# Masks from VectorE, two banks with different head placement, and another order of the first steps in a retention and feed-forward kernel

## The chip, the cores and the metric

The kernel runs on one core of one Trainium2 chip. The metric is device time in microseconds (us) of one execution. Before the change it is 185.12 us, the median of three runs (185.02 to 185.44).

## The reference

Four sequences of 768 tokens, 8 heads of 64. Each head keeps a 64 x 64 state that decays by a factor per step:

```python
gamma = 1.0 - 2.0 ** (-5.0 - np.arange(H))
for t in range(S):
    state = gamma * state + outer(k[:, :, t], v[:, :, t])
    y[:, :, t] = scale * q[:, :, t] @ state
x = y as (3072 tokens, 512)
a = x @ w1;  b = x @ w2            # 512 -> 1024
out = ((a * b) @ w3) @ w_out       # 1024 -> 1024 -> 512
```

Everything goes in and comes out as float32.

## The kernel before

**Tiling.** The 768 tokens of a sequence are cut into three chunks of 256 (`T`, `PER`), so there are 12 chunks, n = 0 to 11. `w3` and `w_out` are multiplied once into a 1024 x 512 matrix `W3O`, so that a chunk needs three products: with W1, with W2 and with W3O. All products run in float16 with float32 sums. The first two chunks (`EO` = 2) hold tokens in pairs per partition and are split in two halves; the later ones are split in four subchunks (s, g), two banks g of two halves s.

**One chunk of attention.** `scores` (L335) makes k times q per subchunk; `mask` (L346, L352) multiplies it on VectorE with a triangle of ones, `keep` or `keep64`, into `am`. `kv` (L374) makes k times v; `state` adds it up on VectorE, and its last step multiplies the end state by the decay of 256 steps, `GS`, on GpSimd (L62). `inter` (L425) writes state times q into two PSUM banks X[n, 0] and X[n, 1], and `av` (L450) adds `am` times v into the same banks. Both are made of small products of 64 rows and 64 columns, so that the 128 x 128 array holds four of them: a row half (the partitions that the operands lie in) and a column half (the partitions that the output goes to). In `inter` head parity r gives both: row half r, column half r. In `av` the row half is g, the column half r. Between the two stands `fence` (L438), a copy on ScalarE of a few columns of each bank, so that `av` starts in a bank only when `inter` is done there. `x_out` (L467; L462 for chunks 0 and 1) multiplies each bank by a table of decays, `YN` or `YS`, into `XT`, one VectorE instruction a bank.

**Numbers and tables.** `numbers` and `late_numbers` write indices with iota on GpSimd, and after them, on GpSimd too: logarithms of the decays by 16 memsets of one column (`LGH`, `LGP`, L148 and L149), the masks by memset and affine selects (`keep`, L152 to L156, and `keep64`, L169 to L172), and `GS` by 8 memsets (L210). VectorE multiplies and converts (`arguments`, `late_arguments`), ScalarE takes exponentials (`tables`, `late_tables`; YN by 4 instructions).

**One chunk of the feed-forward part.** `two_blocks` (L484) makes a quarter of a or b for 256 tokens, 8 products of 256 columns. `a_evac` copies a out of PSUM on ScalarE (L59); `b_evac` multiplies it by b on VectorE into `HT` (L62). `o_unit` (L532) multiplies HT by W3O, 8 products of 512 columns per 128 tokens, and `o_copy` (L546) takes it out on ScalarE. `rows` (L514) is the same work as `two_blocks` for chunks 0 and 1, cut by rows of w1 and w2, so that it can start when the first rows are there.

**W3O.** Per row block f of w3: `cast_w3` to float16, `turn_w3` (8 transposes, L236), `turned_w3` out of PSUM, `w3_mm(f, i)` (2 products of 512 columns with quarter i of w_out, L248; `cast_wo` casts that quarter), `w3_out`. `warm` (L565) multiplies zeros, only to keep TensorE busy.

**What sets the order.** The schedule is manual: each engine executes its instructions in the order in which the program issues them, and waits by semaphores. Up to chunk 4's attention, the order is a list written out by hand (L572 to L841); then a loop over n = 3 to 11 (L879) issues, for each n: `inter(n)`, `fence(n)`, scores and kv of n + 1, `av(n)`, `x_out`, states and masks of n + 1, transposes of chunk n + 2 and loads of chunk n + 3, output products of n - 1, and four units of `two_blocks` and evacuations. Loads come from SP's queue in the order of a list, `fetch` (L120), into 15 buffers of 512 KB: r is a row block of w3, wo a quarter of w_out, w1 and w2 followed by a digit their quarters of rows, q, k and v followed by a digit a chunk. Later chunks' k and q are transposed by DMA, from SP too (`dma_turn`, L295), after a cast on GpSimd.

Of the kernel before, what the change touches and what calls it, by code (L numbers as in the profile page):

```python
# [20 lines left out]
def kernel(  # L21
# [44 lines left out]


# [40 lines left out]
    def fetch(names):  # L108
# [12 lines left out]
        "r3 r6 wo0 r5 q0 r4 wo2 k0 wo1 wo3 r2 v0 r1 r7 k1 q1 v1 w12 w11 r0 w10 w13 w23 w20 w21 w22 "  # L121
        "v2 q2 k2 q5 k3 k4 q3 q4 v3"
# [10 lines left out]
    LGP = const.tile([128, NP], FP, name="LGP")  # L133
    keep = const.tile([128, 2, 128], FP, name="keep")
# [4 lines left out]
    def numbers():  # L139

        nc.gpsimd.iota(key_i[:, :, :], pattern=[[1, 2], [0, H]], base=1 - 128, channel_multiplier=2)
        nc.gpsimd.iota(
            col_i[:, :, :].rearrange("p g (t j) -> p g t j", t=2), pattern=[[128, 2], [1, 2], [2, 64]],
            base=1 - 128, channel_multiplier=0,
        )
        for h in range(H):
            r = (h % 2) * 64
            nc.gpsimd.memset(LGH[:, h : h + 1], -math.log(gam[h]))  # L148
            nc.gpsimd.memset(LGP[r : r + 64, h // 2 : h // 2 + 1], math.log(gam[h]))  # L149

    def keeps():
        nc.gpsimd.memset(keep[:, :, :], 1.0)  # L152
        for g in range(2):
            rows = slice(g * 64, g * 64 + 64)
            for t in range(2):
                nc.gpsimd.affine_select(  # L156
                    out=keep[rows, t, :], in_=keep[rows, t, :], compare_op=GE, fill=0.0,
                    base=-t, pattern=[[1, 2], [2, 64]], channel_multiplier=-2,
                )

    def late_numbers():
# [7 lines left out]
        nc.gpsimd.memset(keep64[:, :], 1.0)  # L169
        for g in range(2):  # L170
            rows = slice(g * 64, g * 64 + 64)
            nc.gpsimd.affine_select(  # L172
                out=keep64[rows, :], in_=keep64[rows, :], compare_op=GE, fill=0.0,
                base=0, pattern=[[1, 2], [2, 32]], channel_multiplier=-1,
            )
# [5 lines left out]
    GS = const.tile([128, NP, 64], FP, name="GS")  # L181
# [13 lines left out]
    def identity():  # L195
        make_identity(nc, ident16[:, :])
# [10 lines left out]
    def step_decays():  # L207
        for h in range(H):
            r, p = (h % 2) * 64, h // 2
            nc.gpsimd.memset(GS[r : r + 64, p, :], gam[h] ** T)  # L210

    def late_arguments():
        tt("v", vn_x[:, :, :], tok_i[:, :, :], lgh(), MULT)
        copy("v", pos_f[:, :, :, :], pos_i[:, :, :, :])

    def late_tables():
        nc.scalar.activation(VN[:, :, :], vn_x[:, :, :], AF.Exp)
        for p in range(NP):
            nc.scalar.activation(YN[:, :, p, :, :], pos_f[:, :, :, :], AF.Exp, scale=LGP[:, p : p + 1])

# [91 lines left out]
    def half(x):  # L312
        return slice(x * 64, x * 64 + 64)

# [63 lines left out]


# [4 lines left out]
    def state(n, i, eng="g"):  # L384
# [3 lines left out]
        if i == len(cs) + 1:  # L388
            if n % PER < PER - 1:
                TS[n + 1, cs[0] if n + 1 < EO else (0, 0)] = t = att.tile([128, NP, 64], HP, tag="t0", name="t0")  # L390
                tt(eng, t[:, :, :], TS.pop((n, "end"))[:, :, :], GS[:, :, :], MULT)
# [18 lines left out]
    def inter(n, tags):  # L410
# [4 lines left out]
        for a in range(NP):  # L415
            for c in cs:
                if (n, c) not in TS:
                    continue
# [13 lines left out]
    def fence(n):  # L432

        for g in range(2):
            if (g, 0) in X[n]:
                s0 = 0 if n < EO or (n, (0, g)) in TS else 1
                t = att.tile([128, NP, 2 - s0], FP, tag=f"fence{g}", name="fence")
                nc.scalar.copy(t[:, :, :], X[n, g][:, :, :].rearrange("p a (s i) -> p a s i", s=2)[:, :, s0:, 0])  # L438

    def av(n):  # L440
        begun = X.pop(n)
        for a in range(NP):
            for t in range(2):
                for g, r in QUARTERS:
# [3 lines left out]
                    else:  # L448
                        o, rhs = X[n, g][half(r), a, t * 64 : (t + 1) * 64], am[n, None, r][half(g), a, t, :]
# [6 lines left out]
    def x_out(n, g):  # L456
# [9 lines left out]
        else:  # L466
            nc.vector.tensor_tensor(  # L467
                XT[n][:, :, :].rearrange("p a (s x) -> p (a s) x", s=2)[:, :, g * 64 : (g + 1) * 64].rearrange(
                    "p k (i t) -> p k t i", t=2
                ),  # L470
                x[:, :, :].rearrange("p a (s t i) -> p (a s) t i", s=2, t=2),
                YN[:, g, :, :, :].rearrange("p a s (t i) -> p (a s) t i", t=2), MULT,
            )
# [100 lines left out]
    identity()  # L574
    step_decays()
    late_numbers()
    numbers()
    warm(3, "F2")
    cast_w3(3, "v")
    turn_w3(3, "S0")  # L580
    keeps()
    late_arguments()
    warm(9, "F2")
    arguments()
    late_tables()
    turned_w3(3, "v")
    cast_w3(6, "g")
    cast_wo(0, "v")
    tables()
    turn_w3(6, "S0")  # L590
    cast_w3(5, "g")
    w3_mm(3, 0, "S1", first=True)
    turned_w3(6, "v")
    w3_mm(6, 0, "S0", first=True)
    turn_w3(5, "X0")
    cast("q", 0, "v")
    warm(2, "F2")
    turned_w3(5, "s")
    turn("q", 0, "X1")
    cast_w3(4, "v")  # L600
    w3_mm(5, 0, "X0", first=True)
    turned("q", 0, "v")
    turn_w3(4, "K")
    warm(3, "F2")
    cast_wo(2, "s")
    turned_w3(4, "v")
    w3_mm(4, 0, "X1", first=True)
    w3_mm(6, 2)
    w3_mm(3, 2)
    cast("k", 0, "v")  # L610
    w3_mm(5, 2)
    turn("k", 0, "K")
    w3_mm(4, 2)
    cast_wo(1, "s")
    turned("k", 0, "v")
    scores(0, ("K", "F0"), 0)
    cast_wo(3, "s")
    w3_mm(4, 1)
    mask(0, 0, 0)
    w3_mm(3, 1)  # L620
    mask(0, 1, 0)
    w3_mm(6, 1)
    cast_w3(2, "s")
    w3_mm(4, 3, last=True)
    w3_mm(3, 3, last=True)
    w3_out(4, "v")
    w3_mm(5, 3)
    w3_out(3, "s")
    turn_w3(2, "K")
    cast_v(0, "v")  # L630
    w3_mm(6, 3, last=True)
    turned_w3(2, "s")
    w3_mm(5, 1, last=True)
    scores(0, ("S1", "X1"), 1)
    w3_out(5, "v")
    kv(0, ("F0", "F1"))
    w3_out(6, "s")
    w3_mm(2, 1, "K", first=True)
    mask(0, 1, 1)
    w3_mm(2, 2)  # L640
    w3_mm(2, 3)
    cast_w3(1, "v")
    cast_w3(7, "s")
    w3_mm(2, 0, last=True)
    state(0, 1)
    turn_w3(1, "S0")
    w3_out(2, "s")
    mask(0, 0, 1)
    inter(0, ("X0", "X1"))
    turn_w3(7, "F0")  # L650
    turned_w3(1, "v")
    fence(0)
    cast("k", 1, "s")
    av(0)
    state(0, 2)
    w3_mm(1, 0, "S0", first=True)
    state(0, 3)
    x_out(0, 0)
    turned_w3(7, "s")
    turn("k", 1, "S1")  # L660
    x_out(0, 1)
    w3_mm(1, 2)
    w3_mm(1, 1)
    cast("q", 1, "s")
    turned("k", 1, "v")
    w3_mm(7, 1, "X0", first=True)
    w3_mm(7, 3)
    turn("q", 1, "S1")
    cast_v(1, "v")
    w3_mm(7, 2)  # L670
    turned("q", 1, "s")
    w3_mm(7, 0, last=True)
    cast_w(W1, "w1", 2, "g")
    kv(1, ("X1", "K"))
    w3_out(7, "s")
    w3_mm(1, 3, last=True)
    state(1, 1)
    scores(1, ("S1", "F0"), 1)
    state(1, 2)
    w3_out(1, "s")  # L680
    scores(1, ("X0", "X1"), 0)
    cast_w(W1, "w1", 1, "g")
    mask(1, 0, 1)
    inter(1, ("F1", "F2"))
    rows(W1, 0, 1, 2, ("S0", "K"), first=True)
    fence(1)
    mask(1, 0, 0)
    state(1, 3)
    rows(W1, 0, 1, 1)
    cast_w3(0, "s")  # L690
    mask(1, 1, 0)
    rows(W1, 0, 0, 1, ("S1", "X0"), first=True)
    rows(W1, 0, 0, 2)
    mask(1, 1, 1)
    turn_w3(0, "X1")
    cast_w(W1, "w1", 0, "v")
    av(1)
    turned_w3(0, "s")
    rows(W1, 0, 1, 0)
    x_out(1, 0)  # L700
    rows(W1, 0, 0, 0)
    x_out(1, 1)
    w3_mm(0, 1, "X1", first=True)
    w3_mm(0, 3)
    cast_w(W1, "w1", 3, "v")
    cast_w(W2, "w2", 3, "g")
    rows(W1, 1, 0, 2, ("F0", "F1"), first=True)
    rows(W1, 1, 0, 1)
    rows(W1, 1, 0, 3)
    cast_w(W2, "w2", 0, "v")  # L710
    w3_mm(0, 0)
    w3_mm(0, 2, last=True)
    rows(W1, 0, 1, 3, last=True)
    w3_out(0, "s")
    rows(W1, 0, 0, 3, last=True)
    rows_out("a", 0, 1, 1, "v")
    cast_w(W2, "w2", 1, "s")
    rows(W2, 1, 0, 0, ("X1", "F2"), first=True)
    rows(W2, 1, 0, 3)
    rows_out("a", 0, 0, 1, "v")  # L720
    rows(W1, 1, 0, 0, last=True)
    rows_out("a", 0, 0, 0, "s")
    cast_w(W2, "w2", 2, "v")
    rows(W2, 1, 1, 1, ("X0", "K"), first=True)
    rows_out("a", 1, 0, 1, "s")
    rows(W2, 1, 0, 1)
    rows_out("a", 1, 0, 0, "v")
    rows_out("a", 0, 1, 0, "s")
    rows(W2, 0, 1, 2, ("S1", "F1"), first=True)
    rows(W2, 1, 1, 2)  # L730
    cast_v(2, "v")
    rows(W2, 0, 0, 1, ("S0", "F0"), first=True)
    rows(W2, 0, 0, 3)
    rows(W2, 0, 0, 2)
    rows(W2, 0, 1, 3)
    cast("q", 2, "g")
    rows(W2, 0, 0, 0, last=True)
    rows(W2, 1, 1, 3)
    rows_out("b", 0, 0, 1)
    rows(W2, 0, 1, 0)  # L740
    rows(W2, 0, 1, 1, last=True)
    rows_out("b", 0, 0, 0)
    turn("q", 2, "F0")
    cast("k", 2, "g")
    rows_out("b", 0, 1, 0)
    rows(W2, 1, 1, 0, last=True)
    rows(W2, 1, 0, 2, last=True)
    turned("q", 2, "v")
    rows(W1, 1, 1, 3, ("S0", "S1"), first=True)
    rows_out("b", 1, 0, 1)  # L750
    rows(W1, 1, 1, 0)
    cast("q", 5, "g")
    rows(W1, 1, 1, 1)
# [201 lines left out]
```

## Time and profile before

| | |
|---|---|
| three runs, median | 185.12 us |
| profiled execution | 185.08 us |
| its span on the core | 183.3 us |
| TensorE busy / weight loads | 175.6 / 126.2 us |
| VectorE, ScalarE, GpSimd busy | 102.3, 67.2, 52.5 us |
| `inter`, chunks 4 to 11, one | 0.56 us, 0.43 in chunks 6 and 9 |
| `x_out`, chunks 2 to 11, one bank | 0.72 us |
| first load landed, first w3 product | 4.7 us, 10.45 us |
| start of the loop's first unit | 74.1 us |

The profile has a page (busy time, share in slices, the chain of work that ended last) and a trace that can be asked for windows, engines and waits. In a row of the timeline stand the start and the duration in us, the engine, the line of the kernel, the operation, what it wrote and read with its shape, a count, and in brackets how long the engine stood idle before it and what ended that. PE is TensorE, PEld its weight loads, DVE VectorE, ACT ScalarE, POOL GpSimd, SPq the queue of SyncE. In the chain a row is a start, a duration, an engine and what it wrote, with the line. A load of 512 KB is 128 rows of 4 KB for weights, but runs of 512 bytes for q and the first chunks, and of 256 bytes for k and v from chunk 2 on.

### The profile page before, as it was taken

What the parts mean: (1) busy time and instruction counts of PE and PEld (TensorE: products, weight loads), DVE (VectorE), ACT (ScalarE), POOL (GpSimd) and SP (SyncE); (2) the same over time, 40 slices, a digit from 0 to 9 for tenths busy, and PEclk for the clock granted to TensorE, in tenths of its full rate; (3) what the DMA queues carried; (4) which work ended last, traced back from release to release, by engine and by line L of the source; (5) the groups of instructions that cost most, each with busy time, mean ns of one, the idle gap of its engine ahead of it and who ended that gap; (6) DMA issues with size and microseconds to landing.
All of it is one profiled execution on the core that took longest, in us unless ns stands there. A gap on an engine that the chain in (4) does not pass through costs nothing.

```text
span 183.3 us, 5995 instructions
## 1 busy us (share of the span) xinstructions
PE 175.6 (96%) x2609; PEld 126.2 (69%) x2609; DVE 102.3 (56%) x173; ACT 67.2 (37%) x126; POOL 52.5 (29%) x82
## 2 busy tenths in 40 slices
PE   7779999999999999999999999999999999999993
PEld 2345455778965875885877858868688587784872
DVE  0544697867595495748357384464654836634320
ACT  2537477626062422332314314233233231331322
POOL 7830004420334005254435334434433400000000
PEclk9969999999999999999999999999999999999999
DMA  5999999996989999689899999999999991200203
GB/s 189 378 361 385 357 287 393 408 320 177 248 193 277 167 181 204 143 186 242 164 251 160 242 180 249 261 206 239 268 229 217 333 382 64 90 28 5 114 0 114
DMA packets 83578, 40.76 MB, mean 222 GB/s; under 512 B 61408, under 2 KB 78048, under 8 KB 83552
## 3 DMA queue, kind: packets, MB, share of 16 engines
q1 hardware_dynamic: 83552, 40.38, 88.0%
q8 instruction: 20, 0.33, 0.8%
q14 instruction: 6, 0.05, 0.1%
HBM read 29.36 MB, written 6.29 MB: 194 GB/s over the span
## 4 chain that ended last, share of the span: by engine, by line
PE 91%; POOL 4%; DVE 1%; issue 1%; ACT 0%; POOLq 0%
PE psF L484 34%; PE psF L532 19%; PE psX L248 4%; PE psS L248 3%; PE psS L514 3%; PE psX L425 3%; PE psF L514 2%; PE psX L532 2%; PE psS L532 2%; PE psX L484 2%; PE psX L450 2%; PE psX L514 1%; PE psS L484 1%; PE psS L335 1%; PE psK L248 1%
## 5 line engine op out<-in xcount | busy, mean ns | idle before, releaser
L484 PEld LDWEIGHTS <-w 128*128 128x128 f16 x640 | 62.5, 98 | 9.4 <-DVE xt L467 0.2
L484 PE MATMUL psF<-xt,w 128*128 128x256 f16 x576 | 64.4, 273 | 0.0
L62 DVE TENSOR_TENSOR ht<-pa,psF 128x512 f16<-128x512 f32 x39 | 26.8, 687 | 43.3 <-PE psF L484 41.1
L532 PE MATMUL psF<-w3o,ht 128*128 128x512 f16 (+2 forms) x168 | 36.4, 369 | 0.0
L59 ACT COPY pa<-psF 128x512 f32<-128x512 f32 x37 | 21.7, 586 | 34.0 <-PE psF L484 33.5
L532 PEld LDWEIGHTS <-ht 128*128 128x128 f16 x200 | 18.5, 98 | 19.5
L546 ACT ACTIVATE st<-psF 128x512 f32<-128x512 f32 (+2 forms) x19 | 10.9, 575 | 30.7 <-PE psF L532 30.7
L62 POOL TENSOR_TENSOR v<-st,VN 128x1024 f16<-128x1024 f32 x8 | 15.2, 1904 | 22.7 <-DMA st<-in_v_dram 22.7
L59 POOL CAST k<-st 128x1024 f16<-128x1024 f32 x9 | 9.3, 1038 | 27.7 <-DMA st<-in_k_dram 23.0
L467 DVE TENSOR_TENSOR xt<-psX,YN 128x512 f16<-128x512 f32 x16 | 10.7, 722 | 6.2 <-PE psX L450 6.2
L514 PEld LDWEIGHTS <-w 128*128 128x128 f16 x128 | 12.2, 98 | 2.1
L59 POOL CAST q<-st 128x1024 f16<-128x1024 f32 x9 | 9.4, 1042 | 13.4 <-DMA st<-in_q_dram 13.4
L62 POOL TENSOR_TENSOR t<-s,GS 128x256 f16<-128x256 f32 x8 | 5.8, 728 | 22.4 <-DVE s L62 22.4
L248 PEld LDWEIGHTS <-w3t 128*128 128x128 f16 x64 | 5.5, 98 | 6.0 <-DVE w3t L59 1.5
L565 PE MATMUL psF<-zeros 128*128 128x512 f16 x25 | 8.1, 466 | 1.3 <-DVE zeros L128 1.3
L248 PE MATMUL psX<-wo,w3t 128*128 128x512 f16 x32 | 8.9, 380 | 0.1
L352 DVE TENSOR_TENSOR am<-psS,keep 128x512 f16<-128x512 f32 x14 | 8.9, 680 | 0.0
L514 PE MATMUL psS<-xt,w 128*128 128x256 f16 x48 | 8.2, 273 | 0.0
L425 PEld LDWEIGHTS <-t 64*64 64x64 f16 x320 | 6.3, 109 | 2.5 <-issue 2.2
L248 PE MATMUL psS<-wo,w3t 128*128 128x512 f16 x24 | 7.1, 400 | 0.4 <-DVE w3t L59 0.4
L236 PEld LDWEIGHTS <-w3h 128*128 128x128 f16 x64 | 4.4, 104 | 4.4 <-POOL w3h L59 2.5
L514 PE MATMUL psF<-xt,w 128*128 128x256 f16 x40 | 6.5, 273 | 0.0
(135 smaller groups left out, 198.3 us busy)
## 6 DMA issues: line engine op xcount, KB each, us to landing
st<-in_moe_w_dram SPq DMA_DIRECT2D x16, 512.0 KB, 8.9
st<-in_q_dram SPq DMA_DIRECT2D x12, 512.0 KB, 6.1
st<-in_v_dram SPq DMA_DIRECT2D x20, 256.0 KB, 6.1
st<-in_k_dram SPq DMA_DIRECT2D x20, 256.0 KB, 4.7
out_dram<-st SPq DMA_DIRECT2D x8, 512.0 KB, 5.1
st<-in_moe_w_out_dram SPq DMA_DIRECT2D x4, 512.0 KB, 8.4
out_dram<-osb SPq DMA_DIRECT2D x3, 512.0 KB, 5.5
st<-in_k_dram SPq DMA_DIRECT2D x2, 512.0 KB, 9.8
```

Of the source, the lines that this page charges most:

```text
L59: {"v": nc.vector.tensor_copy, "g": nc.gpsimd.tensor_copy, "s": nc.scalar.copy}[eng](dst, src)
L62: (nc.vector if eng == "v" else nc.gpsimd).tensor_tensor(dst, a, b, op)
L236: nc.tensor.transpose(ps[:, g * 128 : (g + 1) * 128], src[:, c0 : c0 + 255 : 2], ident16[:, :])
L248: nc.tensor.matmul(acc[f][:, :], lhsT=w3t[f][:, g * 128 : (g + 1) * 128], rhs=WO[i][:, r, :], start=(first and r == 0), stop=(last and r = ...
L352: nc.vector.tensor_tensor(t[:, :, :, :].rearrange("p a s i -> p (a s) i"), ps[:, :, :, :].rearrange("p a s i -> p (a s) i"), keep64[:, :]. ...
L425: nc.tensor.matmul(o, lhsT=TS[n, c][half(r), a, :], rhs=rhs, start=((g, r) not in begun), stop=False, skip_group_check=True,)
L467: nc.vector.tensor_tensor(XT[n][:, :, :].rearrange("p a (s x) -> p (a s) x", s=2)[:, :, g * 64 : (g + 1) * 64].rearrange("p k (i t) -> p k ...
L484: nc.tensor.matmul(ps[:, i, :], lhsT=W[d][:, f * 128 : (f + 1) * 128], rhs=XT[n][:, d, :], start=(i == 0 and d == 0), stop=(i == 1 and d = ...
L514: nc.tensor.matmul(rows_ps[w, n, uh][j // 2][:, j % 2, :], lhsT=W[d][:, f * 128 : (f + 1) * 128], rhs=XT[n][:, d, :], start=(first and j % ...
L532: nc.tensor.matmul(ps[:, :], lhsT=HT[n][:, f, tb * 128 : (tb + 1) * 128], rhs=W3O[f][:, c0:c1], start=(f == 0), stop=(f == 7),)
L546: nc.scalar.activation(o_sb[n][:, tb, c0:c1], o_ps.pop((n, tb, c0, c1))[:, :], AF.Copy, scale=final_scale)
L565: nc.tensor.matmul(ps[:, :], lhsT=zeros[:, 0:128], rhs=zeros[:, :], start=True, stop=True)
```

## The change

Three things are changed. Masks are made by VectorE, as comparisons of index tables, logarithms by memsets on VectorE, and the decay of 256 steps by one exponential of ScalarE (`GS` with one column per pair of heads, broadcast where it is used). From chunk 2 on, heads of the second bank go to the other column half (`place`), `inter` and `av` name their tiles in the order that fits, the second bank's table YN is made with the logarithms of the other head (`LGX`; 8 instructions instead of 4), `x_out` of that bank is two instructions of 64 partitions, the marker copy of that bank is on VectorE in the loop, and the last `b_evac` of a chunk is issued after the next chunk's markers. And `fetch` and the hand-written list have another order, with another distribution of casts and evacuations over the engines; k4 and v4 are loaded after the transposes of chunk 3, q5, k5 and v5 after those of chunk 4, and q4 earlier.

```diff
-        "r3 r6 wo0 r5 q0 r4 wo2 k0 wo1 wo3 r2 v0 r1 r7 k1 q1 v1 w12 w11 r0 w10 w13 w23 w20 w21 w22 "
-        "v2 q2 k2 q5 k3 k4 q3 q4 v3"
+        "r1 r2 wo3 wo2 r3 wo1 wo0 r5 r0 q1 k1 r7 q0 r4 k0 v0 r6 v1 w10 w12 w13 q4 w11 w20 w22 w23 "
+        "w21 v2 k2 q2 q3 k3 v3"
...
+    def logs():
         for h in range(H):
-            nc.gpsimd.memset(LGH[:, h : h + 1], -math.log(gam[h]))
-            nc.gpsimd.memset(LGP[r : r + 64, h // 2 : h // 2 + 1], math.log(gam[h]))
+            nc.vector.memset(LGH[:, h : h + 1], -math.log(gam[h]))
+            nc.vector.memset(LGP[half(h % 2), h // 2 : h // 2 + 1], math.log(gam[h]))
     def keeps():
-        nc.gpsimd.memset(keep[:, :, :], 1.0)
+        copy("v", key_f[:, :], key_i[:, :, 0])
         for g in range(2):
             for t in range(2):
-                nc.gpsimd.affine_select(
+                nc.vector.tensor_scalar(
+                    keep[half(g), t, :], col_f[half(g), g, :], key_f[half(g), t : t + 1], None, op0=GE
...
+    def late_keeps():
+        copy("v", tok_f[:, :], tok_i[:, 0, 0:1])
         for g in range(2):
-            nc.gpsimd.affine_select(
+            nc.vector.tensor_scalar(
+                keep64[half(g), :], pos_f[half(g), g, 0, :], tok_f[half(g), :], None, op0=GE
...
     def step_decays():
-            nc.gpsimd.memset(GS[r : r + 64, p, :], gam[h] ** T)
+        nc.scalar.activation(GS[:, :], LGP[:, :], AF.Exp, scale=float(T))
...
+    def place(n, g, r):
+        return half(r if n < EO or g == 0 else 1 - r)
...
     inter:
-                for r in range(2):
+            for c, r in [(c, r) for c in cs for r in range(2)] if n < EO else [
+                ((s, g), r) for s in range(2) for g, r in ((0, 0), (1, 1), (0, 1), (1, 0))
+            ]:
-                        o, rhs = X[n, g][half(r), a, s * 64 : (s + 1) * 64], qchunk(n, r, a, s, g)
+                        o, rhs = X[n, g][place(n, g, r), a, s * 64 : (s + 1) * 64], qchunk(n, r, a, s, g)
...
     av:
-                for g, r in QUARTERS:
+                for g, r in QUARTERS if n < EO else ((0, 0), (1, 0), (0, 1), (1, 1)):
...
     x_out:
+            for to in (slice(0, 128),) if g == 0 else (half(0), half(1)):
+                at = to if g == 0 else slice(64 - to.start, 128 - to.start)
...
     the list, its first steps:
+    cast_w3(1, "s")
+    numbers()
+    turn_w3(1, "S0")
+    cast_w3(2, "v")
+    turned_w3(1, "v")
+    turn_w3(2, "S1")
+    warm(5, "F2")
+    turned_w3(2, "s")
+    cast_wo(3, "g")
+    logs()
+    arguments()
+    late_arguments()
+    step_decays()
+    tables()
+    cast_wo(2, "g")
+    w3_mm(1, 3, "S0", first=True)
+    late_keeps()
+    w3_mm(2, 3, "S1", first=True)
+    keeps()
+    w3_mm(1, 2)
+    cast_w3(3, "v")
...
     the list, w2's rows and chunk 2:
+    cast_w(W2, "w2", 3, "v")
+    rows(W2, 0, 1, 2, ("X0", "X1"), first=True)
+    cast_w(W2, "w2", 1, "v")
+    rows(W2, 0, 1, 3)
+    rows(W2, 0, 1, 0)
+    rows(W2, 0, 0, 3)
+    rows(W2, 0, 1, 1, last=True)
...
+    dma_turn("q", 3)
+    cast("k", 3, "g")
...
+    dma_turn("k", 3)
+    fetch("k4 v4")
+    dma_turn("q", 4)
...
     the loop:
-            fence(n)
+            fence(n, "v")
+            b_last()
             if nxt and not late:
                 ahead(n + 1)
...
-            b_unit(n, u, tags[(2 * u + 1) % 3])
+            ps = two_blocks(W2, n, u, tags[(2 * u + 1) % 3])
+            b_last = functools.partial(b_evac, n, u, ps)
+            if u < 3 or n == NS - 1:
+                b_last()
```

More of the change, by code (lines that the diff above doesn't have):

```diff
@@ L1 @@
+import functools
 import math
@@ L638 @@
[L638 to L660, printed above, removed]
-    x_out(0, 1)
@@ L662 @@
[L662 to L676, printed above, removed]
+    w3_mm(1, 0, last=True)
+    w3_out(2, "s")
+    w3_mm(3, 0)
+    w3_out(1, "s")
+    w3_mm(3, 2, last=True)
+    cast_w3(0, "g")
+    turn_w3(5, "S1")
@@ L744 @@
[L744 to L749, printed above, removed]
+    inter(1, ("S0", "F0"))
+    w3_out(6, "v")
+    state(1, 3)
+    rows(W1, 0, 0, 0, ("X1", "F1"), first=True)
+    fence(1)
+    av(1)
+    cast("q", 4, "g")
+    rows(W1, 0, 1, 3)
+    x_out(1, 1)
+    rows(W1, 0, 0, 3)
+    x_out(1, 0)
+    rows(W1, 0, 1, 0)
+    rows(W1, 0, 0, 2)
+    cast_w(W1, "w1", 1, "v")
```

413 lines of the change are left out of this document (202 added, 211 removed).

## The prediction

> **What bounds the kernel now.** The page first, for the busy shares and the chain that ended last:
>
> ```profile
> PE 175.6 (96%) x2609; PEld 126.2 (69%) x2609; DVE 102.3 (56%) x173; ACT 67.2 (37%) x126; POOL 52.5 (29%) x82
> ...
> PE 91%; POOL 4%; DVE 1%; issue 1%; ACT 0%; POOLq 0%
> ```
>
> TensorE is the bound, and the one other engine with a share worth naming is GpSimd, 4%. The chain in order of time shows where each of the two sits. The start:
>
> ```profile
> 7.75 1.09 POOL keep L156 x2
> 8.90 1.05 POOL w3h L59
> 9.99 0.64 PE psS L236 x8
> ```
>
> and one turn of the loop (chunk 5; columns: start, duration, what):
>
> ```profile
> 86.11 6.99 PE psF L484 x64
> 93.10 0.56 PE psX L425 x28
> 93.72 0.25 PE psS L335 x26
> ...
> 94.27 0.29 PE psX L450 x32
> 94.56 3.56 PE psF L532 x16
> 98.12 6.99 PE psF L484 x64
> ```
>
> The reader sees two things. GpSimd builds numbers and masks until 8.9, and only then casts the second row block of w3 that TensorE waits for. And the loop is TensorE without a hole: `inter` (L425) 0.56 us, `scores` 0.25, `kv` 0.30, `av` (L450) 0.29, the output product 3.56, the four units 6.99. A saving on TensorE there is a saving of time; a saving elsewhere is none.
>
> Third, the first 74 us, which end where the loop's first unit starts (74.14 in the chain). I count the TensorE work in them by durations from the chain: 14 transposes of 0.46, 32 `w3_mm` of 0.43, 32 `rows` of 0.44, 8 two-block products of 0.87, 6 output products of 1.78, and 6.7 of scores, kv, inter and av: 58.6 us. So 15.5 us of the first 74 are not useful, most before 20 us. What could take their place is the DMA, so the fourth view is windows (last columns: granted clock, DMA share, GB/s):
>
> ```profile
> 12.00:14.00 2.00, 2.00 (x13) 1.22 (x11) 0.61 (x1) 0.68 (x1) 0.00 (x0) 0.50 1.17 326
> ...
> 38.00:40.00 2.00, 2.00 (x17) 1.36 (x14) 2.00 (x4) 0.00 (x0) 1.04 (x1) 1.00 1.10 337
> 40.00:42.00 2.00, 2.00 (x16) 1.39 (x15) 0.60 (x2) 0.45 (x1) 0.00 (x0) 1.00 0.78 162
> ```
>
> The queue is full from 2 to 40 us: loads land one behind the other. When, is read from engines that sat waiting for them:
>
> ```profile
> 4.68 0.69 DVE L59 CAST w3h<-st 128x1024 f16<-128x1024 f32 x1 [3.49 <-DMA st<-in_moe_w_dram]
> ...
> 38.40 1.04 POOL L59 CAST w<-st 128x1024 f16<-128x1024 f32 x1 [3.81 <-DMA st<-in_moe_w_dram]
> ...
> 49.86 1.04 POOL L59 CAST k<-st 128x1024 f16<-128x1024 f32 x1 [2.82 <-DMA st<-in_k_dram]
> ```
>
> The first load landed at 4.7, the 23rd (w2 row 3) at 38.4: 1.53 us each. The 9th and 11th, which ScalarE waited for, landed at 16.2 and 18.9 (1.42 each), and k of chunk 2, the 29th, at 49.8.
>
> **The change, part by part.** All sums go against the profiled execution: 185.08 us, of which 183.3 is its span and 1.8 lies around it; the median of the three runs is 185.12, so the two agree to 0.04.
>
> *Swapped heads, second bank.* In `inter` each quarter tile of the array is a row half times a column half; before, head r goes from row half r to column half r for both banks, so two of the four tiles work: 16 products on each, 0.56 us, 0.035 each. After, heads of bank 1 go to the other column half and the order goes round all four tiles: 8 products on each. `av` is such a round of 32 products of the same size on four tiles, and takes 0.29. So 0.56 becomes 0.28 for chunks 4, 5, 7, 8, 10, 11; chunks 6 and 9 have no carried state (24 products, 0.43), and their fullest tile still has 8, so 0.28. Loop: 6 x 0.28 + 2 x 0.15 = **1.98 us**. Bounds: nothing (tiles disturb each other) to 2.2 (the pace of `scores`, 0.25). `av` only renames its tiles.
>
> On this the Trainium skill, "TensorEngine Tiling (Array Packing)", section Restrictions and Gotchas, speaks against the change: different row tiles cannot access one PSUM bank at the same time. After the change both row halves write into each bank. But so they do before, in every pair of `inter`; one at a time, 32 products at 0.035 would take 1.1 us, and 0.56 was measured, so the trace does not bear the rule out for two halves of one bank. By the rule the sum would lose the 1.98; it stands below as a rival.
>
> *What the swap costs.* `x_out` of the second bank is two VectorE instructions of 64 partitions instead of one of 128; cost goes by columns (the pair now takes 1.34, so 0.65 for one more; at most 0.72). The last `b_evac` now waits behind the marker copy. VectorE after a loop turn's `inter` starts at s: marker ready at s+0.6, copy to s+0.75, `b_evac` 0.69 to s+1.4; then three `x_out` to s+3.4, states 1.7, masks 1.3: s+6.4. TensorE wants XT at s+4.7 (after `av` and 3.56 of output products), the last quarter of HT at s+2.5 (only the seventh of eight products reads it), and the masks and the next `b_evac` at s+6.7. All is covered, by 1.1 us or more except the last, by 0.3; past that, a `b_evac` is late, and its bank is not wanted again for 1.7 us. Cost 0; up to 0.7 a turn if the cover were gone. The marker on VectorE beside ScalarE's runs beside `scores` and `kv` (0.55); in the last chunk, with no cover, TensorE waits for the first marker as before.
>
> *Masks, logarithms.* GpSimd loses 32 small instructions, the last of which ends at 8.8, and is free from about 3. VectorE gets 16 one-column memsets, two conversions, two copies and six comparisons, none of which it shows. Nearest rows: its 16-column product starts 0.1 ahead of the next instruction and lasts 0.17; its 256-column memset lasts 0.27. So 16 memsets cost 1 to 4.3; I take 0.1 each, by the 16-column row, and with the rest 3.7 us, from 7.3 to about 11, just ahead of the cast of row block 3, which lands at 10.3. Late by up to 0.7 here; 3 us if the memsets are dear. ScalarE's tables (4.5 us with eight short ones for YN) end by 14, before it has other work. The state decay by a broadcast operand is GpSimd's 0.73 with 3 us of slack.
>
> *The order of the first steps.* Loads now begin r1 r2 wo3 wo2 r3 wo1 wo0, so every w3 block soon has all its partners. At 1.42 a load: r1 4.7, cast on ScalarE 1.05, transposed by 6.3; r2 6.1; wo3 7.5, cast by free GpSimd, so the first `w3_mm` at 8.5 (10.45 before); wo2, then a hole until block 3 is cast, 11.7; from 12.2 steady work, with a hole of about 0.7 at 16.3 (block 0 lands at 16 and takes 1.04 on GpSimd). By 22 us 12.3 us of useful work are done, against 8.6 before: **3.7 ahead**. But from there data pace it. The same 23 loads (q4 instead of a w2 row) still land by 38.4, then w20 39.9, w22 41.4, w23 42.9, w21 44.4. `rows` with w21 can start at 45.1, after a 0.7 cast, and 27.2 us of the 58.2 us (0.43 less for `inter` of chunks 2 and 3) stand from there: the loop starts at 72.3, plus 0.3 for small waits: 72.6. Before, the last w2 row was used at 44.57, with 29.6 us to go. So of 3.7 us, **1.5 stay**; the rest is spent waiting for w1 and w2. Later data fit: k2 at 49.8 and its cast by 50.9 against a transpose wanted at 50.4; k and q of chunk 4 about when they are wanted. SP is moved as well: q4 is loaded early, k4, v4 and q5 behind transposes, each of which holds SP until its cast is done.
>
> Sum: 185.08 - 1.98 - 1.5 = **181.6 us**.
>
> **Rivals.**
> 1. *The data keep TensorE's pace.* Between 40 and 78 us the DMA share is under 1 in windows that add up to 4.8 us, and 27 loads' worth of bytes have moved by 42. If w21 lands by 42, the start keeps 3.5: 179.6. Against it: landing, not moving, releases the cast, and the 23rd landed 3 us behind its bytes.
> 2. *The start gives nothing*, because VectorE's list ahead of block 3 is dear or waits on k4 and q5 eat the 1.5: 185.08 - 2.0 = 183.1.
> 3. *The four tiles do not overlap*: `inter` stays 0.56, the swap does not do what it is laid out to do: 185.08 - 1.1 = 184.0. Against it: the pairs before, as above. The Trainium skill's rule, from "TensorEngine Tiling (Array Packing)", Restrictions and Gotchas, would give this case.
> 4. *Slower: the late loads take the bound.* From 46.0 (q2) to 60.9 (q4, six loads later) loads landed 2.5 us apart, transposes among them. If loads 24 to 29 came at that pace, k2 would land at 53.4, its transpose start at 54.5 and the loop, 22 us later, at 76.5; with 2.0 won in the loop that is 185.5. This is where it decides: at 2.7 each k2 is 1.2 later, 186.7. Against it: full queue, big rows and 1.5 measured up to the 23rd.
>
> **Chances.** Forecast 0.62 (own range 180.3 to 182.7); rival 1 0.11; rival 2 0.12; rival 3 0.06; rival 4 0.07; nothing measurable, 0.02. A measurement of this kernel tells 0.2% (0.37 us) from no change. The range reaches to rivals 1 and 2: 179.3 to 183.4; rivals 3 and 4 and the tails beyond stay out. Faster: forecast and rivals 1 to 3, less 0.02 for their tails: 0.89; same 0.04, the 0.02 and those tails; slower 0.07.
>
> **What would show it.** Chain of the loop: L425's successor at 0.28 in eight turns, turns of 11.7 us. Chain of the start: no GpSimd masks, first `w3_mm` product near 8.5, loop start near 72.6. Waits: TensorE idle behind casts of w1 and w2 between 33 and 46. VectorE: three `x_out` a chunk, no `ht` wait of TensorE. Wrong would be: L425 still at 0.56, the loop starting after 74, or TensorE waiting for kT of chunk 2 past 51.

## The result, and the profile after

After the change the kernel takes **183.58 us** (median of 20 runs, 182.37 to 186.07) against 185.03 before (20 runs, 183.92 to 186.93): a ratio of 0.9916, 95% interval 0.989 to 0.9942. It is faster, but by 1.5 us where 3.5 were forecast, and the time lies 0.2 above the range. Two later comparisons gave 0.9954 (0.9924 to 0.9984) and 0.9981 (0.9941 to 1.002); the second is not clear of no change. A reason for such differences, which the numbers below need, is this: in a share of the executions TensorE's mean granted clock is about 0.991 instead of 1.0 (48 of 130 of the kernel before, 15 of 44 after), and those take longer, 185.41 against 184.43 before, 185.50 against 183.56 after. So at full clock the change is worth 0.87 us over all these executions (0.65 and 0.59 in the two later comparisons, which have the clock of both kernels), and with the lowered clock nothing. The profiled executions of both kernels (185.08 and 185.5 us, spans 183.3 and 183.7) have the lowered clock.

The page of after, busy shares and the chain's shares by engine:

```profile
PE 174.6 (95%) x2603; PEld 123.9 (67%) x2603; DVE 113.8 (62%) x216; ACT 63.0 (34%) x117; POOL 55.5 (30%) x57
...
PE 91%; DVE 6%; issue 1%; ACT 0%; DVEq 0%; ACTq 0%
```

GpSimd's 4% of the chain have gone, and VectorE has 6% in their place. The chain in order of time shows where:

```profile
8.96 1.07 DVE col_f L60
...
12.13 0.49 DVE keep L162 x2
12.62 0.03 issue
12.65 0.70 DVE w3h L60
13.36 0.05 issue
13.40 1.03 PE psX L244 x8
```

TensorE's third block waits for its cast, and the cast for VectorE's list of numbers and masks, whose last comparison ends at 12.62. The windows of after (the third number from the end is the granted clock) show what follows:

```profile
12.00:14.00 2.00, 0.60 (x6) 0.60 (x7) 1.90 (x5) 2.00 (x8) 0.02 (x1) 0.80 1.01 390
14.00:16.00 2.00, 2.00 (x10) 0.90 (x8) 1.29 (x2) 0.22 (x1) 1.71 (x2) 0.50 1.20 303
...
38.00:40.00 2.00, 1.86 (x53) 1.26 (x52) 0.77 (x2) 0.23 (x2) 1.75 (x3) 1.00 1.03 408
40.00:42.00 2.00, 2.00 (x26) 1.78 (x19) 1.76 (x3) 0.00 (x0) 1.81 (x2) 1.00 1.19 297
```

TensorE works for 0.60 of the two microseconds from 12, and from 13.2 its clock is halved for 3.4 us; before, the same happened from 10.9. From 40 us on it is full. The loop's turn of chunk 5 is now:

```profile
87.23 6.99 PE psF L497 x64
94.21 0.38 PE psX L434 x32
94.59 0.29 PE psS L340 x30
...
95.17 0.29 PE psX L462 x32
95.47 3.56 PE psF L545 x16
```

`inter` (L434) has 0.38 where it had 0.56; the next turn starts at 99.02, 11.79 after this one, where before it took 12.01.

### The profile page after: what moved, and what is told of

It reads as the page before. It is cut to its first block, busy times and chain, and to the rows that moved or that the text cites. A ratio compares the mean times of both kernels' runs of the same rounds, so it can differ in the third digit from the quotient of the medians.

```text
span 183.7 us, 5971 instructions
## 1 busy us (share of the span) xinstructions
PE 174.6 (95%) x2603; PEld 123.9 (67%) x2603; DVE 113.8 (62%) x216; ACT 63.0 (34%) x117; POOL 55.5 (30%) x57
## 4 chain that ended last, share of the span: by engine, by line
PE 91%; DVE 6%; issue 1%; ACT 0%; DVEq 0%; ACTq 0%
PE psF L497 34%; PE psF L545 18%; PE psS L256 4%; PE psS L545 4%; PE psF L578 3%; PE psX L527 3%; PE psS L497 2%; PE psF L527 2%; PE psX L434 2%; PE psX L256 2%; PE psX L462 2%; PE psK L527 2%; PE psS L340 1%; DVE w3h L60 1%; DVE am L351 1%
## 5 line engine op out<-in xcount | busy, mean ns | idle before, releaser
L497 PE MATMUL psF<-xt,w 128*128 128x256 f16 x576 | 64.6, 273 | 0.0
L545 PE MATMUL psF<-w3o,ht 128*128 128x512 f16 (+2 forms) x160 | 34.5, 369 | 0.0
L63 POOL TENSOR_TENSOR v<-st,VN 128x1024 f16<-128x1024 f32 x9 | 17.1, 1903 | 21.7 <-DVE ht L63 9.7
L482 DVE TENSOR_TENSOR xt<-psX,YN 64x512 f16<-64x512 f32 (+1 forms) x28 | 20.4, 728 | 3.1 <-PE psX L462 1.3
L559 ACT ACTIVATE st<-psF 128x512 f32<-128x512 f32 (+2 forms) x19 | 10.9, 575 | 31.7 <-PE psF L545 31.7
L256 PE MATMUL psS<-wo,w3t 128*128 128x512 f16 x48 | 13.1, 399 | 0.7 <-DVE w3t L60 0.3
L357 DVE TENSOR_TENSOR am<-psS,keep 128x512 f16<-128x512 f32 x16 | 10.3, 680 | 0.0
L60 DVE COPY fence<-psX 128x8 f32<-128x8 f32 x8 | 1.3, 167 | 11.3 <-PE psX L434 11.3
L545 PE MATMUL psS<-w3o,ht 128*128 128x512 f16 x32 | 7.6, 380 | 0.0
L527 PE MATMUL psX<-xt,w 128*128 128x256 f16 x48 | 7.2, 273 | 0.0
L63 DVE TENSOR_TENSOR t<-psF,t 128x256 f16<-128x256 f32 x13 | 5.5, 424 | 2.3 <-PE psF L379 1.9
```

Of the source, the lines that this page charges most:

```text
L60: {"v": nc.vector.tensor_copy, "g": nc.gpsimd.tensor_copy, "s": nc.scalar.copy}[eng](dst, src)
L63: (nc.vector if eng == "v" else nc.gpsimd).tensor_tensor(dst, a, b, op)
L256: nc.tensor.matmul(acc[f][:, :], lhsT=w3t[f][:, g * 128 : (g + 1) * 128], rhs=WO[i][:, r, :], start=(first and r == 0), stop=(last and r = ...
L357: nc.vector.tensor_tensor(t[:, :, :, :].rearrange("p a s i -> p (a s) i"), ps[:, :, :, :].rearrange("p a s i -> p (a s) i"), keep64[:, :]. ...
L482: nc.vector.tensor_tensor(xt[to].rearrange("p k (i t) -> p k t i", t=2), x[at, :, :].rearrange("p a (s t i) -> p (a s) t i", s=2, t=2), YN ...
L497: nc.tensor.matmul(ps[:, i, :], lhsT=W[d][:, f * 128 : (f + 1) * 128], rhs=XT[n][:, d, :], start=(i == 0 and d == 0), stop=(i == 1 and d = ...
```

## The experiments

Three numbers are read from each profile: the **loop's start** (first unit of the loop in the chain), **eight turns** (from there to the first unit of chunk 11, in which all eight `inter` lie), and the **clock**. Before: 74.14, 95.61 and 0.991; after: 75.38, 94.74 and 0.991. Each kernel ran in five rounds beside the one before, unless it says otherwise.

### The change again, and its two halves

The changed kernel itself:

> The changed kernel once more, for a second profile and for times beside the kernel before on the same chip. Both theories expect 1.0 to 2.2 us less than the kernel before. Theory A (block 3 of w3 is cast behind VectorE's list of numbers, TensorE stands idle for 2.4 us and its clock drops after that): an execution in which the clock does not drop starts the loop about 2 us earlier than the first profile's 75.4, near 73, with the same hole before block 3. Theory B (the data of w1 and w2 pace TensorE, whatever happens before 20 us): the loop starts within 0.5 us of 75.4 in every execution.

Measured: 184.15 us, ratio 0.9954 (0.9924 to 0.9984); start 74.86 at a clock of 0.991, eight turns 94.67. As the profiled execution has the lowered clock, it does not decide between the two theories; a profile at full clock does, further down (e8: 73.38, near theory A's 73).

The loop's part alone, in the kernel before (swapped heads, marker on VectorE, late evacuation; `fetch`, list and masks as before):

> The kernel before with only the swapped heads, the marker copy on VectorE and the late last evacuation; the first steps, GpSimd's masks and logarithms and the order of loads as before. The forecast's term for the loop was 1.98 us (and 0.43 more for chunks 2 and 3): by it 182.7 to 183.1. From the first profile of the changed kernel the eight turns save only 0.9 us, because inter costs 0.50 from its first instruction to the next kind's first instruction, not 0.56, and VectorE is late in some turns: by that 184.0 to 184.3, when the kernel before takes 185.0.

Measured: 184.40, ratio 0.998 (0.9944 to 1.0016); start 74.51, eight turns 94.46. That is 0.5 less than the kernel before, which the interval does not set apart from nothing.

Order and masks alone:

```diff
-            fence(n, "v")
-            b_last()
+            fence(n)
```
(with `inter`, `av`, `x_out` and YN as before, too)

> The changed kernel with the heads of the second bank where they were, both marker copies on ScalarE and the last evacuation in its old place; the new order and VectorE's masks stay. If the parts add up, this is the kernel before less what the first steps give: by the forecast 1.1 us less (183.9), by the first profile about 0.5 us less (184.5), and its difference to the changed kernel is that of the loop, 0.9 us.

Measured: 185.07, ratio 1.0036 (1.0002 to 1.0071); start 73.22 at full clock, eight turns 96.17. **Order and masks by themselves are no gain**, neither the 1.1 nor the 0.5 that was expected. In the same rounds the whole change took 184.15, 0.92 less; the loop's part is the difference between the two.

### Is it VectorE's list?

Block 3 cast on GpSimd, past the list:

```diff
-    cast_w3(3, "v")
+    cast_w3(3, "g")
```

> The changed kernel with the cast of w3's block 3 on GpSimd, which stands idle from 9.9, instead of behind VectorE's list. Theory A: the cast ends near 11.7 instead of 13.3, the hole of TensorE before it shrinks from 2.4 to under 1 us, the clock stays full more often, and the time falls by 1.0 to 2.5 us against the changed kernel. Theory B: the hole goes but TensorE waits as much longer for later loads, and the time stays within 0.4 us.

Measured: 183.68, ratio 0.9928 (0.9896 to 0.996); start 73.45, eight turns 95.09, full clock in all 12 executions. That is 0.47 below the changed kernel in the same rounds, less than theory A's 1.0. Block 3's transposes start at 11.40 instead of 13.40, and the queue behind the list shows itself once more, in the next thing that waits for VectorE, the cast of wo1 (timeline, TensorE):

```profile
11.40 0.62 PE L244 MATMUL psX<-ident,w3h 128*128 128x128 f16 x8
11.86 0.59 PE L578 MATMUL psF<-zeros 128*128 128x512 f16 x2
14.25 1.02 PE L256 MATMUL psS<-wo,w3t 128*128 128x512 f16 x4 [1.80 <-DVE wo L60]
```

So the list was moved as a whole to where VectorE has nothing to do, ahead of its first cast:

```diff
     numbers()
+    logs()
+    arguments()
+    late_arguments()
+    late_keeps()
+    keeps()
     turn_w3(1, "S0")
     cast_w3(2, "v")
...
```

> After's kernel with VectorE's whole list of numbers (logarithms, conversions, masks) issued ahead of its first cast, where VectorE is idle from 1.1 to 5.7 us. Theory A (the list ahead of block 3 is what the start lost): the list takes 3.7 us without GpSimd's casts beside it and ends by 5.8; block 3 is cast when it lands, at 10.3 to 11.0, its transposes start near 11.2 instead of 13.4, a hole of about 0.9 stays for the cast of wo1 (lands 11.9), the clock stays at 1.0, the loop starts at 72.2 to 72.6, and the median is 182.4, ratio 0.986. Theory B (the data pace TensorE up to the loop): the loop starts at 74 or later as in after and the median is 183.5 to 184, ratio 0.993.

Measured: 183.24, ratio 0.9928 (0.9895 to 0.9961); start **72.24**, full clock in all 12. The list runs from 1.08 to 5.13, and block 3 is cast when it lands (timeline, VectorE):

```profile
2.24 0.30 DVE L60 CAST col_f<-col_i 128x256 f32<-128x256 int32 x1
...
2.85 0.34 DVE L60 COPY LGX<-LGP 64x4 f32<-64x4 f32 x2
...
9.61 0.69 DVE L60 CAST w3h<-st 128x1024 f16<-128x1024 f32 x1 [2.56 <-DMA st<-in_moe_w_dram]
```

The start is 3.1 earlier than in after's profile, 1.1 earlier than in the one at full clock (73.38, e8 below), and where it was expected. What TensorE waits for now is the load of block 4: in the window 24 to 26 it is busy for 0.96 of 2.00, and GpSimd casts block 4 at 23.94, when it lands. The time was expected at 182.4. As the start is as foretold, what is missing lies behind it: a pause of 0.64 in the loop, below, is a part, and the rest stays open.

And the masks back to GpSimd, order and loop as after:

```diff
-            nc.vector.memset(LGH[:, h : h + 1], -math.log(gam[h]))
+            nc.gpsimd.memset(LGH[:, h : h + 1], -math.log(gam[h]))
...
+    keeps()
     turn_w3(1, "S0")
...
-    logs()
...
-    late_keeps()
...
-    keeps()
```

> After's kernel with the logarithms and the masks back on GpSimd, as before has them (the decay of 256 steps stays on ScalarE); order of the steps and the loop as after. Theory A: GpSimd's list ends at about 7.4, just when wo3 has landed (7.5), so it holds nothing up, and VectorE is free for block 3 at 10.3: the same start as with the list issued first, loop start 72.2 to 72.8, median 182.4 to 182.8, ratio 0.986 to 0.988; the move of the masks to VectorE was then a loss in this order. Rival (GpSimd's masks are in the way, as they were before): wo3's cast starts 1.3 later than 7.55, first w3 product near 10, loop start 73.4 or later, median 183.6 or more.

Measured: 183.23, ratio 0.9913 (0.9886 to 0.994); start 72.91, full clock in all 12. GpSimd's list ends at 6.49, and its cast of wo3 then waits for the load until 7.66: in this order the masks held up nothing on GpSimd, and their move to VectorE bought nothing. The start is 0.5 earlier than after's at full clock (73.38, e8 below), with the time of the list issued first.

### The clock

TensorE's hole filled, in after and in before:

```diff
+    warm(11, "F2")
     turn_w3(3, "X0")
```

> After's kernel with 11 products of zeros, 0.21 us each, put into TensorE's hole ahead of block 3's transposes (13.40). Theory A (the hole of 2.4 us is what lowers the granted clock, and the lower clock is what some executions lose): the clock is 1.0 in the windows 12 to 18, no execution has a mean clock under 0.996, the loop still starts at 74.2 to 74.9 because the hole is only filled, and the median is that of after's executions at full clock, 183.5 (ratio 0.992). Theory B (the clock drops for another reason, or costs nothing): windows under 0.9 stay, and the median is after's own 184.1. Beside it: the pause of TensorE inside av of chunk 9, after 18 of 32 products, sits 11 products earlier in the program's order if it belongs to a place in TensorE's instruction stream, and stays where it is if it belongs to the data.

Measured: 184.52, ratio 0.9989 (0.9958 to 1.0019). All 12 executions at 0.997 or above, every window from 8 to 18 at 1.00; start 74.24, eight turns 95.38 with a pause of 0.79. So the hole does lower the clock, but the time was missed by 1.0. The profiled execution, 185.19, has pauses of 0.63 and 0.79; that such pauses took the 1.0 in the others as well is not shown.

```diff
+    warm(9, "F2")
     turn_w3(6, "S0")
```

> The kernel before, with 9 products of zeros (0.21 us each) put into TensorE's hole of 2.0 us ahead of its second block's transposes. Theory A (a hole of about 2 us with few products around it lowers the granted clock in some executions): the clock is 1.0 in every window from 8 to 18 us and no execution has a mean clock near 0.991; the loop starts at 72.9 to 73.4 instead of 74.1, and the median is that of before's executions at full clock, 184.3 to 184.5 (ratio 0.997). Rival (the drops come from elsewhere): a third to a half of the executions stay at 0.991, loop start 74.1, median 184.9.

Measured: 185.42, ratio 1.0041 (1.0011 to 1.0071); full clock in all 12, start 73.80. The fill ended at 10.98, and GpSimd's cast had ended by 9.93: it was 1.0 too long. With 5 products:

> The kernel before with 5 products of zeros in TensorE's hole instead of the 9, whose last ended 1.0 us after GpSimd's cast had (10.98 against 9.93) and so delayed the start. If the lowered clock is all that sets the profiled execution of before (loop start 74.14) apart from its executions at full clock, the loop starts at 72.9 to 73.3 here, no execution has a mean clock near 0.991, and the median is 184.2 to 184.5, ratio 0.997. If the start is late for another reason, it is 73.8 or more again and the median 185.

Measured: 184.86, ratio 1.0001 (0.997 to 1.0032); full clock in all 12, start **73.01**, as expected; eight turns 96.27. That is as near as these profiles come to the start of the kernel before without the loss by the clock. But the median was expected at 184.2 to 184.5 and missed. Filling the hole ended the lowered clock in all 36 executions of the three filled kernels, and in none of them did the time fall clear of noise. The kernel before, unchanged, for one more profile:

> The kernel before, unchanged, for one more profile. At full clock (about 6 in 10 executions) the loop starts at 72.9 to 73.4 and the execution takes 183.9 to 184.6; at a mean clock of 0.991 it starts at 74.1 and takes 185.1 to 185.9.

Measured: 185.1, clock 0.988, start 73.78. And the changed kernel a third time:

> The changed kernel once more, on one chip with the two below. If the list's place is worth what the loop starts show (75.4 and 74.9 in after's profiled executions, 72.2 with the list first), its median is 1.5 to 2 above that of the kernel with the list first; if most of that difference was the lowered clock of the two profiled executions, its executions at full clock are only 0.3 to 0.7 above it.

Measured: 185.33, ratio 0.9981 (0.9941 to 1.002), with the clock lowered in 8 of 12 executions. The profiled one is at full clock and takes 183.87: start **73.38**, eight turns 95.09. The kernel with the list first took 183.24, in other rounds on another chip; the four executions at full clock of this one have a median of 183.9. So most of the distance between the two starts first seen, 75.4 and 72.2, was the lowered clock, and 1.1 of it the list.

### The pauses in the loop

In several profiles TensorE stops in the middle of a run of products, and the chain names it "issue": no wait of an engine stands behind it. In after and in e1, e3, e4, e6, e7, e8 and e10 this comes after 2141 products, and in e5 after 1757, three times 128 fewer. To tell a place in the program from a place in TensorE's stream of instructions, the stream was shifted, in the kernel with the list first. `small(m)` makes m products of zeros of 64 columns; 44 of them stand in place of 6 of `warm`'s:

```diff
-    warm(8, "F2")
+    small(16)
+    warm(6, "F2")
...
-    warm(5, "F2")
+    warm(3, "F2")
+    small(15)
...
-    warm(2, "F2")
+    small(13)
```

> The kernel with the list first, and 38 more products in TensorE's instruction stream: 44 small ones of zeros (64 columns each) in place of 6 of the large ones of zeros, put where TensorE waits in the first 12 us, so that its work is not later. Theory C (the holes of TensorE that nothing explains, 0.64 at 139.3 us with the list first, stand where a packet of its instructions, 16 KB, 128 products, comes late): a hole, if there is one, again stands after 2141 products or a multiple of 128 away from it, so 38 products earlier in the program, inside kv of chunk 10, or in another place of that row; its size may differ, 0 to 0.8, and with it the median by as much, 182.6 to 183.3. Rival (the hole belongs to that place of the program, av of chunk 9): it stays after 18 of the 32 products of av in chunk 9, after 2179 products, 0.6 long, median 183.2.

Measured: 184.62, ratio 0.998 (0.9946 to 1.0013); start 72.64, eight turns 96.29. The median was expected at 182.6 to 183.3, and is missed. Three pauses, of 0.21 (ahead of the loop), 0.94 and 0.63, in other places than before; the products executed up to each (windows from the span's start, TensorE; the number after x):

```profile
0.00:71.41 71.41, 67.83 (x989) 1.00 1.07 291
0.00:92.53 92.53, 88.74 (x1373) 1.00 1.11 272
0.00:153.85 153.85, 149.12 (x2397) 1.00 1.13 254
```

and the second of them in the chain, inside `av` of another chunk:

```profile
92.34 0.19 PE psX L462 x20
92.53 0.94 issue
93.47 0.29 PE psX L462 x12
```

989, 1373 and 2397 are 349 + 128 x 5, x 8 and x 16; 2141 and 1757 are x 14 and x 11. The old loop has them at the same counts (e10 at 2141, e13 0.16 us at 1758). So they belong to the stream, in steps of 128 products. The page's queue line says of what size its parts are (packets, MB):

```profile
q8 instruction: 20, 0.33, 0.8%
```

0.33 MB in 20 packets is 16 KB each, and 2603 products over 20 packets are about 130 a packet. That these packets hold TensorE's instructions, 128 products with their weight loads each, is read from the two sizes, and the times bear it out. The trace has the start and duration of every packet, 0.88 to 1.97 us in all profiles. In each of the 17 pauses found, the products after border 349 + 128 x k go on 1.2 to 1.5 us after packet k + 2 of this queue has landed: in e6 packet 16 lands at 138.45 and the products go on at 139.94, in e9 packet 10 lands at 92.19 and they go on at 93.47. At no border of the 16 profiles does the next product start sooner than 1.2 us after its packet. So a pause is a wait for instructions, at the borders that TensorE reaches before that. Why those packets come late is argued, not shown: in the loop the pauses stand 8.1 to 9.2 us after a turn's first unit, in or just behind some 120 small products that are used up in 1.3 us, about as long as a packet takes. The faster `inter` makes that stretch denser.

Shifted by 4 products only:

```diff
     warm(5, "F2")
+    small(4)
```

> The kernel with the list first, and 4 more small products of zeros where TensorE waits for wo3's cast. Theory C (a packet of 128 products that is late): packet borders fall 4 products earlier in the program, so in chunk 9 after 14 of the 32 products of av, and in chunk 7 inside the output products; a pause is possible at either and at no other place of the loop but after 349 products and multiples of 128; its size is not foretold, 0 to 0.9. Median 182.6 without a pause, 183.2 with one as long as 0.64.

Measured: **183.15**, ratio 0.9909 (0.9878 to 0.994), 9 executions; start 72.96 and no pause in the loop: eight turns 94.17, the fewest of all. The profiled execution took 182.71, but the median is 0.5 above what was expected without a pause; pauses of other executions are not seen. It has the lowest median here, but not clear of the 183.24 without the shift.

The old loop with the list first, to have the loop's worth in the other setting:

> The kernel with the list first, with the loop's part of the change undone (swapped heads, marker on VectorE, late evacuation). Theory: the new loop saves 0.18 a turn, not 0.28, 1.0 to 1.4 over the kernel: the loop starts at 72.1 to 72.6, turns take 11.95, the span is 182.1 to 182.4 and the median 184.2 to 184.6. Rival (the loop saves what was predicted, 1.98): median 185.2; rival (holes eat all the loop's gain): median 183.3.

Measured: 185.09, ratio 1.0014 (0.998 to 1.0048); start 73.80, eight turns 96.59 with a pause of 0.62 after 2141 products. The time is nearest to the first rival's 185.2, but half of the distance between this profile and e6's (spans of 184.0 and 181.0) lies ahead of the loop: the start is 1.2 later than foretold. Up to 72 us TensorE is busy for 1.1 less than in e6 (66.56 against 67.65), all of it ahead of 36 us; why stays open. The eight turns take 1.58 more than e6's. Over all profiles, eight turns take 95.61 to 96.59 with the old loop (six, mean 96.1) and 94.17 to 96.29 with the new one (ten, mean 95.0).

## Why the prediction was wrong, step by step

**The loop: right in mechanism, too large by 0.4 to 0.9.** The step that failed is "So 0.56 becomes 0.28". The four tiles do overlap, as the products of chunk 5 show, before and after:

```profile
93.03 0.63 PE L425 MATMUL psX<-qT,t 64*64 64x64 f16 x28
93.47 0.22 PE L335 MATMUL psS<-qT,kT 64*64 64x64 f16 x2
...
93.53 0.19 PE L425 MATMUL psX<-qT,t 64*64 64x64 f16 x1
93.56 0.42 PE L335 MATMUL psS<-qT,kT 64*64 64x64 f16 x28
```

```profile
94.14 0.45 PE L434 MATMUL psX<-qT,t 64*64 64x64 f16 x32
94.42 0.46 PE L340 MATMUL psS<-qT,kT 64*64 64x64 f16 x32
```

After the change the 32 products of `inter` take 0.28 until the first of `scores`, as predicted. But measured in that way they took 0.44 before, and 0.50 to the last of them, which stands among the first of `scores`; not 0.56. A piece of the chain ends where its last product ends, 0.19 after that product's start, and after the change that piece is 0.38. The prediction took the old size from one measure and the new one from another. A turn saves 0.2. Eight turns save 1.44 if the best profile of each loop is taken (95.61 less 94.17), 1.58 between e10 and e6, and 1.1 as a mean over all profiles; 1.98 was forecast. The profiles differ by their pauses, and by smaller waits: after's own is 0.57 above the best with a pause of only 0.07.

**"Different row tiles", rival 3, fell.** By the Trainium skill's rule, "TensorEngine Tiling (Array Packing)", Restrictions and Gotchas, both row halves writing into one bank at a time would have left `inter` at its old size. The trace does not agree: 32 products in 0.28, with both row halves in both banks.

**What the swap costs: right.** The three `x_out` take 2.21 where two took 1.35, 0.86 more and not 0.65, but the cost is covered. The late `b_evac` and the three `x_out` were given a cover of 0.3. In the turn of chunk 5 VectorE ends its masks at 100.86 and then still waits 0.19 for TensorE; once, in the next turn, the units take 7.15 instead of 6.99.

**The start: this step failed.** It was forecast to give 1.5, and it gives nothing: 73.38 against 73.01 at full clock (e8, e13, one profile each), 74.9 to 75.4 against 73.8 to 74.1 with the clock lowered. Of the 1.5, 1.1 was a loss by the clock in the execution that the sum went against (74.14 against 73.01), below, and the start at full clock is 0.8 later than the 72.6 of the sum. For this second part, "with the rest 3.7 us" and "Late by up to 0.7 here" are where it went wrong. The first w3 product is at 8.64 (8.5 predicted), the memsets are cheap, 16 in 1.0 us. But the list takes 4.9 us, from 7.74 to 12.62, and block 3, which GpSimd could take at 10.30 in e4, is cast at 12.65 instead of 11. Conversions were priced by rows of VectorE alone, while GpSimd's casts, which the new order puts beside them, hold them up. The two rows in after, VectorE's and GpSimd's:

```profile
8.88 1.16 DVE L60 CAST col_f<-col_i 128x256 f32<-128x256 int32 x1
```

```profile
8.85 1.04 POOL L60 CAST wo<-st 128x1024 f16<-128x1024 f32 x1 [0.26 <-DMA st<-in_moe_w_out_dram]
```

Without a cast beside it (e6) the same conversion takes 0.30; beside one, an instruction on VectorE ends about when GpSimd's cast does. The Trainium skill has the rule, "SBUF — State Buffer", Who interferes with whom: GpSimd shares a pair of ports with VectorE, and a VectorE instruction that uses this pair and one of GpSimd exclude each other for a whole instruction. The trace agrees: 0.86 of the 1.2 by which the list is longer than predicted is this one row, while the memsets beside the GpSimd cast before it (7.55 to 8.59) keep their 0.06.

**The lowered clock was in the prediction's own fence and was not priced.** The window 12 to 14 of before shows 0.50. The sum went against an execution that had lost about 1.0 by it (74.14 against 73.01), and counted a start after a full-clock path as won from it. The change does not take the loss away; TensorE's hole is still there, in before and in after:

```profile
9.99 0.62 PE L236 MATMUL psS<-ident,w3h 128*128 128x128 f16 x8 [2.00 <-POOL w3h L59]
```

```profile
13.40 1.03 PE L244 MATMUL psX<-ident,w3h 128*128 128x128 f16 x8 [2.44 <-DVE w3h L60]
```

The executions with the lowered clock are 1.0 longer than the others before and 1.9 longer after (185.50 against 183.56), although both profiles have the same 3.4 us at half clock; why is not shown.

**"From there data pace it": half right.** With the list out of the way the loop starts at 72.2 to 73.0 (e6, e7, e9, e12), around the 72.6 that was forecast, and at 73.8 in e10. But the loads that bind are not w1 and w2: TensorE is full from 40 us on. It waits at 24 to 26 for block 4, and rival 1's 70.6 never came. Rival 2, the list, gave 183.1, and the measured 183.58 is 0.5 above it; it has the right step for the start, but it kept the whole 2.0 of the loop. Rival 3's 184.0 is as near, by luck: its mechanism fell.

**The sum at full clock:** the loop's 1.1, less 0.4 at the start, is 0.7; measured were 0.6 to 0.87. As the starts of two kernels that differ in 4 small products already lie 0.7 apart (72.24 in e6, 72.96 in e12, one profile each), the closeness is partly luck.

## What to carry to other kernels

Take both sizes of a changed piece by one measure, from first instruction to the next kind's first, since a chain's piece is cut at the ends of products and holds more. When small work moves to another engine, ask which cast is queued behind it there and which engine's casts run beside it; here the idle time ahead of VectorE's first load and the old place on GpSimd were equally cheap (183.24 and 183.23). And look at the granted clock of the execution that a sum goes against: a loss in it that comes and goes is no gain to be had.

## What was not expected of the hardware

**The clock.** A hole of about 2 us at 8 to 13 us cost some executions half the clock for about 3.4 us: in the profiled one of after the windows from 12 to 18 have 0.80, 0.50 and 0.84, which is 2 x (0.20 + 0.50 + 0.16) = 1.7 us of clock lost, or 3.4 us at half. The same kernel with the same hole runs through at 1.00 in other executions (e8, hole 1.84), and e4's hole of 1.80 lowered the clock in none of 12. What sets the profiles apart is in the trace's record of the clock. It changes in steps of 3.41 us, whose borders lie elsewhere in each execution. In the five profiles with a lowered clock (before, after, e1, e2, e14) TensorE worked for 1.02 to 1.52 us in the step just ahead of the lowered one; in the other eleven, with the steps counted on from the record's first change, it worked for at least 1.90 in every step of this stretch, in e8 because a border cuts the hole (2.05 and 2.44 in the two steps). So what decided is how much of the hole fell into one step, and not its length alone. The Trainium skill, "TensorE: Matmul & The Clock Gate", Part 1, has windows of 3413 ns that run freely and do not start with the kernel; the traces agree. By the Trainium skill the clock goes down after at least one idle window; here a window with 1.0 to 1.5 us of work was enough, and the measurement decides.

**Pauses at packet borders of instructions,** 0.07 to 0.94 us, at 349 products and multiples of 128 further, not seen in what engines wait for, but in the times of the packets. Their size differs between executions of one kernel (0.07, 0.17 and 0.28 at 2141 products in after, e1 and e8), and two kernels that differ in 4 products of zeros differ in them (e6 and e12, one profile each). Such a pause, up to 0.94 us, is half a percent of the time.

**VectorE beside GpSimd.** Instructions of 0.2 to 0.3 us took 1.0 to 1.2 when they met a cast of GpSimd: `col_f` 1.16 in after, `vn_x` 1.01 and the two of `LGX` 1.08 in e4, `pos_f` 1.13 in e5, the two of `LGX` 1.14 in e7.
